# Attention and Fourier mixing on one core: the first batch's Fourier stage cut into halves, and the start of the program laid out anew

## The chip, the core and the metric

One core of a Trainium2 chip runs the whole program. The metric is the time of one execution in device microseconds, the median of several runs. The engines are TensorE (PE, with PEld for its weight loads), VectorE (DVE), ScalarE (ACT) and GpSimd (POOL); SyncE (SP) issues most of the DMAs. Each engine works through its own instructions in order and waits on semaphores for the others.

## What is computed

Two stages, in fp32 at input and output. First attention in chunks of 32 positions, each of which sees 8 memory keys, 16 positions to the left and 8 to the right; then a Fourier mixing of the result, and a two-layer network on the normalised sum:

```python
for c in range(S // 32):                       # q, k, v: (4, 8, 768, 64)
    k_full = concat([mem_k, k[c*32-16 : c*32+40]])
    a = softmax(q[c*32 : c*32+32] @ k_full.T / 8)
    attn[c*32 : c*32+32] = a @ v_full
x = attn.transpose(0, 2, 1, 3).reshape(4, 768, 512)
u = x + real(fft(fft(x, axis=1), axis=2))
un = (u - mean(u)) / sqrt(var(u) + 1e-6)
out = u + relu(un @ w_ch1) @ w_ch2             # (512, 2048), (2048, 512)
```

## The kernel before

**Attention.** The work goes in 16 units, four for each of the four batches; a unit `n` is a pair of heads. For a unit the kernel loads q, k and v (`qf`, `kf`, `va`, three buffers each), casts q and k to bf16 (`qb`, `kb`), turns each with eight TensorE transposes (`trq`, `trk`), and copies them out of PSUM (`qT`, `kTb`). Then come two halves `g` of six 64-position tiles each: scores `sc` (12 matmuls), exp into `e` on ScalarE, values `xa` (12 fp32 matmuls, 24 in the profile), and a normalisation on VectorE (`zs`, L360, and `xsb`, L361) into the batch's `xsb`. A key block is 96 wide: 8 memory keys, 16 left, 64 own, 8 right, on partitions 0 to 95. The pairs come in the order 0, 2, 1, 3, so that columns that are added to each other are there early.

**Fourier stage**, by batch (`fourier`, L646). The column sums and differences `zy` (L374), the row fold `pq` (L381, L382: the upper three row tiles plus and minus the lower three) and the column fold `ff` (L391, against a reversed copy) leave four parts (`par`, `ab`) of 128 columns each. ScalarE and VectorE split every part into two fp16 halves (`hi` L399, `lo` L404), and TensorE sums the rows against cosine and sine tables (`ps`, L414, 12 matmuls a part and 12 more for the middle column). The result is split again (`up` L426 and L430, `dn` L435), `pm` (L446) does the columns, VectorE adds and takes mean and variance (L452, L458), ScalarE subtracts the mean (`un`, L464), and `un` is turned, on TensorE for batch 0 (`tp`) and by a DMA for the others.

**Network**, by batch and half `sh`: `ph` (L497, 64 matmuls), a ReLU on ScalarE (L504), `pc` (L511, 48 matmuls), the sum `osb` (L517) and the store.

**Order.** Everything is a task of a planner (`Plan`, `plan.add`): an engine, a cost in us, the tasks it comes after, buffers that it takes and gives, a rank. `order` lets time run over these costs and starts on every engine the task of lowest rank that could start; the emitted program then has that order on every engine, whatever happens on the chip. Network tasks have very high ranks (`MLPS`), so they fill TensorE where nothing else can start. TensorE's costs count double before 40 us. The sine tables (`e_all_sines`) and the DMAs of the network's weights come after the exp of batch 0's last half (`x_last`). `xsb` has three buffers, so batch 3's attention waits for the end of batch 0's network.

Of the kernel before, what the change touches and what calls it, by code (L numbers as in the profile page):

```python
# [21 lines left out]
OWN = NMEM + LEFT  # L22
WIN = OWN + 64 + RIGHT

# [12 lines left out]
class Plan:  # L37
# [4 lines left out]
    LAG = {"PE": 0.2, "DMA": 2.0}  # L42

# [4 lines left out]
    def add(self, engine, cost, emit, after=(), take=(), give=(), rank=None, moved=0.0,  # L48
            loose=False):
        t = dict(engine=engine, cost=cost, emit=emit, after=[a for a in after if a is not None],  # L50
                 take=take, give=give, rank=len(self.tasks) if rank is None else rank,
                 moved=moved, done=None, at=None, no=len(self.tasks), loose=loose)
        self.tasks.append(t)
        return t

    def order(self):
# [8 lines left out]
        while any(waiting.values()):  # L65
# [4 lines left out]
            for e, ts_ in waiting.items():  # L70
# [3 lines left out]
                for t in ts_:  # L74
                    if held and not t["loose"]:
                        continue
                    if any(a["done"] is None or a["end" if a["engine"] == e else "done"] > now
# [11 lines left out]
                    cost = t["cost"] * (2.0 if e == "PE" and now < 40.0 else 1.0)  # L89
                    idle[e] = t["end"] = now + cost  # L90
                    if t["moved"]:
                        wire = max(wire, now + cost) + t["moved"]
                        t["done"] = t["end"] = wire + self.LAG["DMA"]
# [9 lines left out]
            if not moved:  # L103
                times = ([v for v in idle.values() if v > now] + [g[0] for g in gives]
                         + [t["done"] for t in placed if t["done"] > now])
# [8 lines left out]
def kernel(  # L114
# [41 lines left out]
    kf = [spool.tile([KP, 2, RB * D], FP32, name=f"kf{i}") for i in range(NS)]  # L156
    NV = 3
    va = [spool.tile([WIN, 2, NT, 66], FP32, name=f"va{i}") for i in range(NV)]
    NKT = 2
    kTb = [spool.tile([P, NT, WIN], BF16, name=f"kTb{i}") for i in range(NKT)]  # L160
# [27 lines left out]
    ident_b = cpool.tile([P, P], BF16)  # L188
    hpi_b = cpool.tile([P, 1], FP32)
# [4 lines left out]
    sinS = wpool.tile([P, 2, 3, NK], FP16)  # L194
    cosD = wpool.tile([P, 2, HD], FP16)
# [16 lines left out]
    def e_masks():  # L212
        nc.gpsimd.memset(mbias, 0.0)
        nc.gpsimd.memset(mbias[64:WIN, 0:1], NEG)
        nc.gpsimd.affine_select(out=mbias[0:64, 1:2], in_=mbias[0:64, 1:2],
                                compare_op=ALU.is_ge, fill=NEG, base=-(NMEM + CHUNK),
                                pattern=[[0, 1]], channel_multiplier=1)
        nc.gpsimd.memset(mbias[0:NMEM, 1:2], 0.0)
# [5 lines left out]
    def e_edges(i):  # L224
        v1 = va[i]
        nc.vector.memset(v1[:, :, :, D:D + 1], 1.0)
        nc.vector.memset(v1[0:32, :, 0, 0:D], 0.0)
        nc.vector.memset(v1[64:WIN, :, NT - 1, 0:D], 0.0)

    def e_edge_ones(i):  # L230
        v1 = va[i]
        lo, hi = v1[0:32, :, 0, D:D + 1], v1[64:WIN, :, NT - 1, D:D + 1]
        nc.gpsimd.affine_select(out=lo, in_=lo, compare_op=ALU.is_ge, fill=0.0, base=-OWN,
                                pattern=[[0, 2], [0, 1]], channel_multiplier=1)
        nc.gpsimd.affine_select(out=hi, in_=hi, compare_op=ALU.is_ge, fill=0.0,
                                base=OWN - 1, pattern=[[0, 2], [0, 1]], channel_multiplier=-1)
        nc.gpsimd.memset(v1[0:NMEM, :, 0, D:D + 1], 1.0)

    def e_kzero(i, lo, eng):
        r0, r1 = (0, KOFF) if lo else (QP, KP)  # L240
        eng.memset(kf[i][r0:r1].rearrange("p h e -> p (h e)"), 0.0)
# [10 lines left out]
    def e_load_qk(n, i):  # L252
        b, pr = seq[n]
        src, dst = ((q, qf), (k, kf))[i]
        r0 = KOFF * i
        nc.sync.dma_start(dst[n % NS][r0:r0 + QP],
                          src[b, 2 * pr:2 * pr + 2].rearrange("h (p j) d -> p h (j d)", j=RB))

    def e_cast(n, i, eng):
        src, of, rows, tag = ((qf, qb_of, QP, "qb"), (kf, kb_of, KP, "kb"))[i]  # L260
        of[n] = apool.tile([rows, RB, 2, D], BF16, tag=tag, bufs=1, name=tag)
# [3 lines left out]
    def e_load_v(n):  # L265
# [11 lines left out]
        for hh in range(2):  # L277
            run(NMEM, OWN - NMEM + 64, 1, NT - 1, 64 - LEFT, hh)
            run(OWN + 64, RIGHT, 0, NT - 1, 64, hh)
            nc.sync.dma_start(v1[0:NMEM, hh, :, 0:D],  # L280
# [16 lines left out]
    def e_turn_k(n):  # L297
        kb = kb_of.pop(n)
# [5 lines left out]
        for j in range(RB):  # L304
            nc.tensor.transpose(trk[:, j * KP:(j + 1) * KP],  # L305
                                kb[:, j].rearrange("p h d -> p (h d)"), ident_b[0:KP, 0:KP])

    def e_mkT(n):
        b, pr = seq[n]
        nc.vector.tensor_copy(  # L310
            kTb[n % NKT][:, :, 0:NMEM],
            mkT[:, b * HP + pr, :].unsqueeze(1).to_broadcast([P, NT, NMEM]))

    def e_kT(n):
        nc.scalar.copy(  # L315
            strided(kTb[n % NKT], NMEM, [[WIN, NT], [RB, 11], [1, RB]]),
            strided(tr_of.pop((n, 1)), 0, [[64 // RB, NT], [1, 11], [KP, RB]]))

    def e_scores(n, g):
        qT, kT = qT_of[n], kTb[n % NKT]  # L320
        sc_of[n, g] = sc = aps.tile([P, 2, 8, 64], FP32, tag="sc", bufs=1, name="sc")
        for t6 in range(6):
            t = 6 * g + t6
            for hh in range(2):
                r0 = 64 * hh
                nc.tensor.matmul(sc[0:WIN, hh, t6, :], kT[r0:r0 + 64, t, :],  # L326
# [3 lines left out]
    def e_exp(n, g):  # L330
        sc = sc_of.pop((n, g))
        e1_of[n, g] = e1 = apool.tile([WIN, 2, 6, 64], FP32, tag="e1", bufs=3, name="e1")
        for half in range(2):
            nc.scalar.activation(e1[:, :, :, ts(half, 32)], sc[0:WIN, :, 0:6, ts(half, 32)],  # L334
                                 AFT.Exp, bias=mbias[0:WIN, half:half + 1],
                                 scale=1.0 / math.sqrt(D))

    def e_values(n, g):
        e1 = e1_of.pop((n, g))
        if n < HP and g == 1:  # L340
            xa = fps.tile([P, 3, 2, 66], FP32, tag="mlp", name="xa")
        else:
            xa = aps.tile([P, 3, 2, 66], FP32, tag="xa", bufs=1, name="xa")
# [24 lines left out]
    mu_of, unT_of, rstd_of = {}, {}, {}  # L368
# [64 lines left out]
    def e_dn(b, par, ab):  # L433
        dn = fpool.tile([P, 2, HS], FP16, tag="dn", bufs=4, name="dn")
        nc.vector.tensor_copy(dn, rev_ap(up_of[b, par, ab][2], HS, HS, [[2 * NK, 2]]))  # L435
        up_of[b, par, ab][1] = dn

# [86 lines left out]
    t_zero = add("DVE", 0.2, e_zero)  # L524
    t_iota = add("POOL", 0.7, e_iota)
    t_mkf = add("ACT", 0.2, e_mkf, moved=0.8)
    t_id = add("POOL", 0.5, lambda: make_identity(nc, ident), rank=12)
    t_scales = add("DVE", 0.2, e_scales, [t_iota])
    t_kz, t_ones = {}, {}
    for i in range(NS):  # L530
        t_kz[i] = [add("DVE", 0.9, lambda i=i: e_kzero(i, 1, nc.vector), rank=-1) if i == 0 else
                   add("POOL", 0.9, lambda i=i: e_kzero(i, 1, nc.gpsimd), rank=17),
                   add("POOL", 0.9, lambda i=i: e_kzero(i, 0, nc.gpsimd),
                       rank=-1 if i == 0 else 17)]
# [248 lines left out]
```

## Time and profile before

| what | us |
|---|---|
| median of 3 runs (337.01 to 339.83) | 337.48 |
| the profiled execution, its own time | 336.54 |
| its span, first to last instruction | 334.8 |
| TensorE busy | 289.2 (86%) |
| VectorE busy | 177.3 (53%) |
| ScalarE busy | 164.6 (49%) |
| GpSimd busy | 48.9 (15%) |
| mean granted TensorE clock | 0.982 |

Shares are over the whole span, and the program has two unlike parts: up to some 80 us batch 0 goes through attention and Fourier stage, and after that TensorE has network work beside the other batches. In the rows of a timeline stand start, length, engine, line, operation, and in brackets how long the engine was idle before and for whom; in the chain of waits start, length and what ran; in the table by stretch each engine's busy time with its count, then the granted clock, the DMA share and GB/s.

### The profile page before, as it was taken

Reading aid. Unit: us, or ns where it says so; the run is one execution under the profiler, and the core shown is the slowest. Engines: PE = TensorE matmul, PEld = TensorE weight load, DVE = VectorE, ACT = ScalarE, POOL = GpSimd, SP = SyncE. Lnnn points to the kernel's source line nnn. Section 1 sums busy time; section 2 is a strip of 40 time slices with the busy share of each in tenths; the row PEclk is TensorE's granted clock in tenths of the full one; section 3 lists DMA queues with packets and bytes.
Section 4 is the critical chain, followed back from the end, with each engine's and each line's share of the span. In section 5 each row is a group of like instructions: output and inputs, shape, how many; then the busy total and the mean of one; then the engine's idle time right before and its main releaser. Section 6 shows DMA issues by size and latency. Waiting matters only on the chain.

```text
span 334.8 us, 6729 instructions
## 1 busy us (share of the span) xinstructions
PE 289.2 (86%) x2761; PEld 187.1 (56%) x2761; DVE 177.3 (53%) x341; ACT 164.6 (49%) x290; POOL 48.9 (15%) x66
## 2 busy tenths in 40 slices
PE   0585847798999997978999996889999999999995
PEld 0464746676666674656745654655455454554542
DVE  5944169988599894998923369790110200101001
ACT  1364488556796546758525623246345062250620
POOL 8201471013333024320001000000010000000000
PEclk9999999899999999979999999799999999999999
DMA  8999899994999196980054200100420100101001
GB/s 168 208 217 197 180 226 205 198 216 118 206 184 162 55 224 129 232 139 3 2 113 117 29 2 2 40 23 33 108 80 2 63 32 31 65 2 63 31 33 63
DMA packets 60287, 35.18 MB, mean 105 GB/s; under 512 B 48480, under 2 KB 50528, under 8 KB 60256
## 3 DMA queue, kind: packets, MB, share of 16 engines
q1 hardware_dynamic: 53824, 24.19, 38.8%
q0 software_dynamic: 2688, 4.19, 6.9%
q10 hardware_dynamic: 3744, 6.36, 5.1%
q8 instruction: 22, 0.36, 0.5%
q14 instruction: 9, 0.07, 0.1%
HBM read 30.28 MB, written 6.29 MB: 109 GB/s over the span
## 4 chain that ended last, share of the span: by engine, by line
PE 68%; DVE 16%; ACT 7%; DMA 4%; issue 1%; SPq 1%; POOL 0%; ACTq 0%; POOLq 0%; DVEq 0%
PE pc L511 24%; PE ph L497 22%; PE xa L350 7%; PE ps L414 6%; PE pm L446 4%; ACT e L334 3%; PE sc L326 2%; DVE ff L391 2%; DVE lo L404 2%; DVE zy L374 2%; DMA mkf<-in_mem_k_dram 1%; DMA qf<-in_q_dram 1%; DMA unT<-un 1%; DVE xsb L361 1%; DVE pq L381 1%
## 5 line engine op out<-in xcount | busy, mean ns | idle before, releaser
L497 PE MATMUL ph<-unT,w_sb 128*128 128x384 f16 x512 | 92.1, 326 | 1.7 <-ACT hT L504 1.2
L504 ACT ACTIVATE hT<-ph 128x384 f16<-128x384 f32 x128 | 60.9, 490 | 65.2 <-PE ph L497 65.1
L511 PE MATMUL pc<-w_sb,hT 128*128 128x512 f16 x384 | 85.8, 379 | 0.0
L517 DVE SCALAR_TENSOR_TENSOR osb<-pc,rstd,xsb 128x512 f32<-128x512 f32 x24 | 18.0, 749 | 101.7 <-PE pc L511 101.7
L497 PEld LDWEIGHTS <-w_sb 128*128 128x128 f16 x512 | 48.1, 97 | 35.1 <-issue 6.2
L511 PEld LDWEIGHTS <-hT 128*128 128x128 f16 x384 | 37.2, 98 | 42.6 <-issue 0.3
L334 ACT ACTIVATE e<-sc,mbias 96x384 f32<-96x384 f32 x64 | 33.4, 571 | 22.2 <-PE sc L326 21.5
L350 PE MATMUL xa<-va,e 96*64 96x65 f32 x768 | 35.3, 252 | 10.2 <-ACT e L334 9.4
L350 PEld LDWEIGHTS xa<-va,e 96*64 96x64 f32 x768 | 30.4, 162 | 17.4 <-ACT e L334 10.4
L464 ACT ACTIVATE un<-xsb,mu_s 128x512 f16<-128x512 f32 x24 | 17.3, 720 | 29.1 <-DVE mu_s L459 9.1
L262 POOL CAST qb<-qf 96x1024 bf16<-96x1024 f32 x12 | 14.2, 1184 | 82.1 <-DMA qf<-in_q_dram 82.1
L360 DVE RECIPROCAL zs<-xa 128x6 f32<-128x6 f32 x32 | 6.1, 192 | 31.2 <-PE xa L350 31.1
L414 PE MATMUL ps<-cosS,hi 128*128 128x193 f16 (+1 forms) x72 | 16.6, 282 | 4.8 <-DVE ff L391 3.2
L414 PE MATMUL ps<-cosS,lo 128*128 128x193 f16 (+1 forms) x72 | 16.4, 282 | 4.8 <-DVE lo L404 4.8
L326 PE MATMUL sc<-qT,kTb 64*96 64x64 bf16 x384 | 16.9, 228 | 3.8 <-ACT kTb L315 2.0
L426 ACT CAST up<-ps 128x386 f16<-128x386 f32 x16 | 9.6, 603 | 18.7 <-PE ps L414 18.6
L326 PEld LDWEIGHTS <-kTb 64*96 64x96 bf16 x384 | 13.2, 141 | 9.8 <-issue 4.7
L361 DVE TENSOR_TENSOR xsb<-xa,zs 128x384 f32<-128x384 f32 x32 | 17.8, 557 | 1.1
L315 ACT COPY kTb<-trk 128x1056 bf16<-128x1056 bf16 x16 | 16.6, 1036 | 3.7 <-PE trk L305 3.7
L374 DVE TENSOR_TENSOR zy<-xsb 128x768 f32<-128x768 f32 x16 | 17.4, 1098 | 0.3
L414 PEld LDWEIGHTS <-lo 128*128 128x128 f16 (+1 forms) x120 | 13.3, 110 | 7.2 <-DVE lo L404 6.4
L452 DVE TENSOR_TENSOR xsb<-pm,xsb 128x512 f32<-128x512 f32 x24 | 16.0, 667 | 2.2 <-PE pm L446 2.2
(86 smaller groups left out, 316.0 us busy)
## 6 DMA issues: line engine op xcount, KB each, us to landing
va<-in_v_dram SPq DMA_DIRECT2D x32, 220.0 KB
qf<-in_q_dram SPq DMA_DIRECT2D x16, 384.0 KB
kf<-in_k_dram SPq DMA_DIRECT2D x16, 384.0 KB
out_dram<-osb ACTq DMA_DIRECT2D x24, 256.0 KB
w_sb<-in_moe_w_ch_dram POOLq DMA_DIRECT2D x8, 512.0 KB, 15.8
va<-in_mem_v_dram SPq DMA_DIRECT2D x32, 24.0 KB
va<-in_v_dram SPq DMA_DIRECT2D x32, 22.0 KB
va<-in_v_dram SPq DMA_DIRECT2D x16, 32.0 KB
```

The lines of the kernel that those rows point to most:

```text
L315: nc.scalar.copy(strided(kTb[n % NKT], NMEM, [[WIN, NT], [RB, 11], [1, RB]]), strided(tr_of.pop((n, 1)), 0, [[64 // RB, NT], [1, 11], [KP, ...
L326: nc.tensor.matmul(sc[0:WIN, hh, t6, :], kT[r0:r0 + 64, t, :], qT[r0:r0 + 64, ts(t, 64)], start=True, stop=True, tile_position=(r0, 0))
L334: nc.scalar.activation(e1[:, :, :, ts(half, 32)], sc[0:WIN, :, 0:6, ts(half, 32)], AFT.Exp, bias=mbias[0:WIN, half:half + 1], scale=1.0 / ...
L350: nc.tensor.matmul(xa[64 * half:64 * half + 64, st, hh, 0:65], e1[:, hh, t6, :], v1[:, hh, 6 * g + t6, 0:65], start=True, stop=True)
L361: nc.vector.tensor_tensor(xs[b][:, 3 * g:3 * g + 3, 2 * pr * D:(2 * pr + 2) * D] .rearrange("p s (h d) -> p s h d", h=2), xa[:, :, :, 0:D] ...
L374: nc.vector.tensor_tensor(zy_of[b, par][:, :, c0:c0 + P], xb[:, :, c0:c0 + P], xb[:, :, HD + c0:HD + c0 + P], ALU.add if par == 0 else ALU ...
L414: nc.tensor.matmul(out_[:, sp, :], part[:, ab, sp * 3 + st, c0:c1], tab[:, sp, st, :], start=(st == 0 and i == 0), stop=(st == 2 and i == 1))
L464: nc.scalar.activation(un, xs[b][:, kt, :], AFT.Identity, bias=mu_of[b][:, kt, 0:1], scale=-1.0)
L497: nc.tensor.matmul(ph[:, 0:384], w1_sb[:, dt, ts(ht, P)], unT_of[b][:, dt, sh * 384:(sh + 1) * 384], start=(dt == 0), stop=(dt == NDT - 1))
L504: nc.scalar.activation(hT_of[b, sh][:, ht, :], ph_of.pop((b, sh, ht))[:, 0:384], AFT.Relu, bias=0.0, scale=-1.0)
L511: nc.tensor.matmul(pc_of[b, sh, stl], hT_of[b, sh][:, ht, ts(stl, P)], w2_sb[:, ht, :], start=(ht == 0), stop=(ht == NHT - 1))
L517: nc.vector.scalar_tensor_tensor(osb, pc_of.pop((b, sh, stl)), rstd_of[b][:, st:st + 1], xs[b][:, st, :], ALU.mult, ALU.add)
```

## The change

**Key blocks** are 128 wide. Partitions 0 to 31 of a block are zero, then 8 memory keys, 16 left, 64 own, 8 right. The zeros are written once (`va`, `kTb`), and the zero rows that the keys need at the edges come from a shifted identity (`turn_b`) and a cleared strip of a single `kb`, in place of cleared strips of three `kf`.

**Start.** GpSimd makes all casts of q and k. The angles of the tables come first on VectorE and the sines first on ScalarE; negated tables (`odd`, `nsinD`) are made on GpSimd. The kT copy of units 1 to 3 is on VectorE. The weights wait for the load of unit 3's v (`e_gate`). The values of batch 0 use one PSUM buffer instead of two and have later ranks.

**Batch 0's Fourier stage** (`first_fourier`) goes by row half `g` and column quarter: `g_zy` after units 0 and 1, a first fold step after unit 2, a second after unit 3, each of 3 row tiles. The row fold is not made; TensorE sums over both halves, with the table of odd frequencies negated for the second half, and the middle column has its own small part (`g_mid`). That is 120 row matmuls for 60.

**Planner.** A TensorE task that is not network work may be placed up to 0.7 us (`SLACK`) before its inputs are due, after 45 us; the double cost lasts until 45 us. ReLUs, output sums and stores have the lowest ranks instead of the highest.

```diff
+    FIRST = 45.0
+    SLACK = 0.7
...
+                    slack = (self.SLACK if e == "PE" and now > self.FIRST and not t["filler"]
+                             else 0.0)
...
+                           or (a["end"] > now if a["engine"] == e else a["done"] > now - slack)
...
-    kTb = [spool.tile([P, NT, WIN], BF16, name=f"kTb{i}") for i in range(NKT)]
+    kTb = [spool.tile([P, NT, P], BF16, name=f"kTb{i}") for i in range(NKT)]
...
+        nc.gpsimd.memset(v1[0:MEM0].rearrange("p h t c -> p (h t c)"), 0.0)
...
+    def g_ff(par, ab, g, last):
...
+        nc.vector.tensor_tensor(ff[:, :, 1:P], (ff if last else zy)[:, :, 1:P],
+                                rev_ap(xb, 2 * P - 1 + HD * last, P - 1, [[DM, 3]]),
+                                ALU.add if plus else ALU.subtract)
...
+    def g_rows(par, ab, g):
...
+        for sp in range(2):
+            tab = odd[:, ab] if g == 1 and sp == 1 else (cosS, sinS)[ab][:, sp]
...
+            part = [(ps[:, sp, :], g_hl(par, i)[:, ab, 3 * g + st, :], tab[:, st, :])
+                    for st in range(3) for i in range(2)]
...
-        ce, cn, cc = (nc.vector, "DVE", 0.68) if first else (nc.gpsimd, "POOL", 1.04)
+        cq, ck = [add("POOL", 1.1, lambda i=i, e=e: e_cast(n, i, nc.gpsimd), [e], take=(("qb", "kb")[i],),
...
-    t_sines = add("ACT", 6.2, e_all_sines, [t_angle["S"], t_angle["D"], x_last])
-    t_rows = add("DVE", 1.3, e_table_rows, [t_sines])
+    t_sines = add("ACT", 6.9, e_all_sines, [t_angle["S"], t_angle["D"]], rank=SINES)
+    t_neg = add("POOL", 1.4, e_negatives, [t_sines], rank=100)
+    t_rows = add("POOL", 1.8, e_table_rows, [t_sines, t_neg], rank=101)
...
+    t_gate = add("POOL", 0.1, e_gate, [t_lv[HP - 1]])
...
-    done = {0: fourier(0)}
+    done = {0: first_fourier()}
```

ScalarE at the start of the program, before (`trq` and `trk` are the turned q and k, `e` an exp; the sines stand after batch 0's last exp):

```order
L294 ACT_TABLE_LOAD
L294 COPY qT<-trq 128x768
L315 COPY kTb_85<-trk 128x12x88
L334 ACTIVATE e_225<-sc,mbias 96x12x32 x2
L334 ACTIVATE e_279<-sc,mbias 96x12x32 x2
```

and with the change:

```order
L710 ACT_TABLE_LOAD
L710 ACTIVATE sinS<-rS 128x579
L711 ACTIVATE cosS<-yS,hpi_b 128x579
L710 ACTIVATE sinS<-rS 128x579
L711 ACTIVATE cosS<-yS,hpi_b 128x579
L713 ACTIVATE sinD<-tri 128x512
L714 ACTIVATE cosD<-tri,hpi_b 128x512
L306 COPY qT<-trq 128x768
L326 COPY kTb_85<-trk 128x12x88
L306 COPY qT<-trq 128x768
L345 ACT_TABLE_LOAD
L345 ACTIVATE e_292<-sc,mbias 128x12x32 x2
```

All sines moved ahead of the first copy, one of the seven went to GpSimd, and the load of the exp's table stands after the second unit's qT.

GpSimd with the change, from the clear of the second `kTb` to the key cast of unit 1 (`_76`, `_79` are unit 0's buffers, `_77`, `_80` unit 1's); ahead of these rows stand the clears of `kb`, two `va` and the first `kTb`. In before its first cast is one of batch 1:

```order
L627 MEMSET kTb_86 128x1536
L274 CAST qb<-qf_76 96x2x8x64
L270 CAST kb<-kf_79 96x2x8x64
L244 AFFINE_SELECT va_84<-va_84 32x2
L246 AFFINE_SELECT va_84<-va_84 32x2
L249 MEMSET va_84 8x2
L250 MEMSET va_84 32x1584
L274 CAST qb<-qf_77 96x2x8x64
L270 CAST kb<-kf_80 96x2x8x64
```

The casts came over from VectorE, behind the clears, and TensorE's transposes of unit 1's keys, which wait for the last of these rows, stand ahead of its first scores.

VectorE at the end of batch 0's attention, before (from the last normalisation on):

```order
L360 RECIPROCAL zs<-xa 128x6
L361 TENSOR_TENSOR xsb_283<-xa,zs 128x3x128
L374 TENSOR_TENSOR zy<-xsb_283 128x6x128
L381 TENSOR_TENSOR pq<-zy 128x768
L382 TENSOR_TENSOR pq<-zy 128x768
L390 COPY ff<-pq 128x6
L391 TENSOR_TENSOR ff<-pq 128x6x127
```

and with the change, from the normalisation of unit 3's first half:

```order
L368 RECIPROCAL zs<-xa 128x6
L369 TENSOR_TENSOR xsb_341<-xa,zs 128x3x128
L471 TENSOR_TENSOR ff_552<-ff_552,xsb_341 128x3x127 x2
L497 TENSOR_TENSOR mid_114<-xsb_341 128x3
L499 CAST mid<-mid_114 128x3
L500 TENSOR_TENSOR mid<-mid_114,mid 128x3
L491 TENSOR_TENSOR lo_659<-ff_552,hi_658 128x384 x2
L368 RECIPROCAL zs<-xa 128x6
L369 TENSOR_TENSOR xsb_341<-xa,zs 128x3x128
```

The first half's folds and splits stand ahead of the last normalisation, and `pq` is gone.

276 lines of the change are left out of this document (196 added, 80 removed).

## The prediction

> **What bounds the kernel now.** I read the page first, for where TensorE is not full.
>
> ```profile
> span 334.8 us, 6729 instructions
> PE   0585847798999997978999996889999999999995
> DMA  8999899994999196980054200100420100101001
> ```
>
> A digit is 8.4 us. TensorE is loosely filled for nine slices, with the DMA engines full, and nearly solid after them. The chain of waits shows what each part is made of, and where the borders lie.
>
> ```profile
> 44.21 1.28 ACT L617
> 63.53 3.76 PE ps L414 x23
> 67.32 0.62 ACT up L426
> 78.88 0.65 PE ph L497 x4
> 310.05 10.40 PE ph L497 x64
> 320.45 10.37 PE pc L511 x48
> 330.85 0.75 DVE osb L517
> ```
>
> At 44.2 ScalarE begins on the sine tables: a table load of 1.28, seven activations, and a load back; batch 0's row sums end at 67.3, and the first MLP matmul starts near 78.7. From there the chain is mostly TensorE, up to 330.85, and 3.95 us of tail follow. So the time is the start of the MLP, plus the TensorE work still to do then, plus what TensorE loses, plus the tail. The work has these prices at full clock:
>
> ```profile
> 78.54 0.34 PE trq L289 x8
> 88.00 0.39 PE sc L326 x12
> 89.99 0.46 PE trk L305 x8
> 118.35 0.85 PE xa L350 x24
> 203.27 1.02 PE ps L414 x12
> 222.74 0.87 PE pm L446 x8
> ```
>
> In the order of before, after the first `ph` stand 21 groups of `xa`, 18 `sc`, 8 `trq`, 9 `trk`, 15 of twelve `ps`, 18 `pm`, 512 `ph` and 384 `pc`: 17.9+7.0+2.7+4.1+15.3+15.7+83.2+83.0 = 228.9, and under 1 for two `tp`: 229.7 us. The stretch is 330.85-78.7 = 252.2, so 22.4 us are lost in it. A table by stretch (TensorE's busy time is the number after the length), and the rows of the worst place, say where:
>
> ```profile
> 140.00:150.00 10.00, 7.61 (x85) 5.91 (x82) 9.35 (x11) 5.72 (x12) 3.96 (x3) 0.83 1.00 157
> 200.00:210.00 10.00, 6.65 (x53) 4.34 (x50) 9.85 (x16) 4.07 (x6) 0.00 (x0) 1.00 0.01 2
> 209.63 0.26 PE L414 MATMUL ps<-cosS,hi 128*128 128x193 f16 x1 [3.24 <-DVE ff L391]
> 210.63 0.34 PE L414 MATMUL ps<-cosS,lo 128*128 128x193 f16 x1 [0.73 <-DVE lo L404]
> ```
>
> The last batch's 60 row matmuls stand in one piece, with MLP work behind them: TensorE waits 4.0 us for VectorE, and then runs some 24 of them at half clock (163 ns each, 3.76 over 23, for 85), 1.9 us more.
>
> **The change, part by part.** I follow the path to the first `ph`.
>
> *Head.* GpSimd now casts all of q and k, and before that clears a `kb` strip, two `va` blocks (1584 elements) and two `kTb` (1536). Its nearest rows:
>
> ```profile
> 0.79 0.95 POOL L241 MEMSET kf<- 4x1024 f32 x1 [0.29 <-POOLq L767]
> 5.55 4.69 POOL L241 MEMSET kf<- 2x1024 f32 x4
> 13.65 1.04 ACT L334 ACTIVATE e<-sc,mbias 96x384 f32<-96x384 f32 x2 [0.86 <-PE sc L326]
> 14.75 1.57 PE L350 MATMUL xa<-va,e 96*64 96x65 f32 x24 [1.21 <-ACT e L334]
> 16.25 0.69 PE L326 MATMUL sc<-qT,kTb 64*96 64x64 bf16 x12
> 16.87 0.82 PE L289 MATMUL trq<-ident_b,qb 96*128 96x96 bf16 x8
> 17.92 0.79 ACT L294 COPY qT<-trq 128x768 bf16<-128x768 bf16 x1
> 19.58 0.85 PE L305 MATMUL trk<-ident_b,kb 100*128 100x100 bf16 x8
> 32.24 1.03 POOL L262 CAST qb<-qf 96x1024 bf16<-96x1024 f32 x1 [22.00 <-DMA qf<-in_q_dram]
> ```
>
> A memset costs 0.95 per 1024 elements, 1.17 in the row of four. Before reaches 5.55 with one such memset behind it; less that and the third `va` block's small pieces (0.6) it is 4.0. Then the strips take 0.95+2x1.47+2x1.42 = 6.7, so the first cast begins near 10.7; two casts (2.1), the third `va` block (2.0) and two casts more bring pair 1's key cast to about 17. If two-byte clears take half it is 15; with 1.17 for 0.95 and casts at 1.2, 20. TensorE has pair 1's `trk` ahead of the first scores, so they all stand behind that cast. Then `trk` 0.85, `trq` 0.82, the qT copy 0.8 (scores beside it), the Exp table 1.28, exp 1.04, second scores 0.69: `xa` starts at 22.5, where before has 14.75. The sines fill that hole: ScalarE has no copy to make until some 12 us. They cost nothing while VectorE has the angles by 10; each us later moves qT, and soon the path, by one.
>
> *Attention.* From there TensorE is the bound, at half clock:
>
> ```profile
> 34.15 1.50 PE xa L350 x24
> 35.65 0.64 PE sc L326 x10
> 25.32 0.69 DVE L262 CAST qb<-qf 96x1024 bf16<-96x1024 f32 x1 [3.64 <-DMA qf<-in_q_dram]
> 46.09 0.56 DVE L361 TENSOR_TENSOR xsb<-xa,zs 128x384 f32<-128x384 f32 x1
> 46.90 1.63 POOL L262 CAST qb<-qf 96x1024 bf16<-96x1024 f32 x1
> 47.67 1.67 DVE L381 TENSOR_TENSOR pq<-zy 128x768 f32<-128x768 f32 x1
> 63.67 0.94 DVE L404 TENSOR_TENSOR lo<-ff,hi 128x768 f16<-128x768 f32 x1
> L391 DVE TENSOR_TENSOR ff<-pq 128x762 f32<-128x762 f32 x16 | 15.0, 941 | 0.0
> ```
>
> Eight `xa` (12.0), six `sc` (3.8), five transposes (4.0), and 2.3 of standing for VectorE, since `xa` now has one PSUM buffer and the normalisation of 0.8 lies between: the last `xa` ends at 44.6. Before it ends at 45.8. The head's loss is won back because pair 2's values no longer stand behind a transpose that waits for batch 1's q, and the loads arrive in time (q of pair 3 landed at 25.3 in before).
>
> *Fourier stage.* The normalisation of pair 2's first half ends at 22.5 + 7.5 (five `xa`) + 2.6 (four `sc`) + 3.2 (four transposes) + 0.9 (itself) = 36.7. After it VectorE has sixteen half-size fold steps (0.5 each, 8.0), their small copies (1.2), eight `lo` (0.5 each, 4.0), the middle column (0.9) and three normalisations (2.3): 16.4, to 53.1. The casts of pair 5 fall on it. A cast took 1.63 instead of 1.03, and `pq` 1.67 instead of the 0.94 of `lo`, which has its size, when they met (rows above); I add 1, half of what three such meetings cost: 54. Before, the last `lo` ends at 64.6. The Trainium skill (SBUF — State Buffer, § Who interferes with whom) says that a VectorE operation with two SBUF inputs contends with a GpSimd instruction that reads SBUF, which speaks against casts on GpSimd here; the two stretched rows agree with it, and by it all folds that meet a cast pay, 2 us instead of 1. The kT copies of pairs 1 to 3, now VectorE's (ScalarE's took 1.0), fall before 36.7, where it waits for `xa`: nothing, or 1 where one stands ahead of a normalisation.
>
> The row fold `pq` is gone from VectorE and comes back as 60 more matmuls. TensorE starts the 120 at 45.6: 21 at half clock (3.5), 99 at 85 ns (8.4), scores and values of pair 4 between (1.3): 58.8, after VectorE's 54 plus 2, so TensorE is late next. If the clock stayed half throughout it would be 66. From the last row sum to the first `ph` before takes 78.7-67.3 = 11.4, of which two normalisations (0.75 each) drop out of VectorE's row: 10.2. The MLP starts at 69.0, 9.7 earlier.
>
> *Weights.* Their eight DMAs stand on GpSimd's queue behind a gate copy that waits for pair 3's v, and behind pair 4's casts; the casts of pair 5 stand behind them.
>
> ```profile
> L640 POOL DMA_DIRECT2D w_sb<-in_moe_w_ch_dram x4: 560/566/801, 41.5 to 43.4; - x4
> DMA to landing us min/median/max: 7.9/11.2/14.4
> ```
>
> Pair 4's keys are cast by 38; issued to 41 and 14.4 on the way, w1 is there at 55: hidden by 14 us.
>
> *After that.* The new order has 22 `xa`, 20 `sc`, 10 `trq` and 10 `trk` groups behind the first `ph`, 2.8 us more: 232.5. MLP work now stands between the pieces of the last batch's row sums, so the 5.9 us there should go; lost time 22.4-5.9 = 16.5, and 1.5 for waits that the planner's slack (0.7 us) now allows: 18. Key blocks of 128 columns: a scores group moves as many columns as before; if its loads grew by a third, 0.11 x 20 = 2.2 us; if they hide, nothing, and a faster load could give up to 1. I take nothing, since `trq` has 128-column loads already and eight of them fit with their matmuls into 0.34. Zero rows, exp on 128 partitions, tables on GpSimd: same lengths or beside other work, nothing.
>
> **Sum.** 69.0+232.5+18+3.95 = 323.4 of span. The profiled execution takes 336.54 for its span of 334.8, and the median is 0.94 above it: 323.4+1.74+0.94 = 326.
>
> **Rivals.** *The head eats the gain.* GpSimd at its worst prices and casts that meet VectorE's angle operations put pair 1's keys at 23; everything moves by 6, and with the stalls of the last batch kept (6) the result is 338, with half of either 332. For it: the clears already stretch from 0.95 to 1.17 in before. Against: the fold chain, not the attention, is the longer of the two, and part of a late head is lost in its waits. Within 1%: chance 0.14.
>
> *Planned waits (slower).* After 45 us the planner places a non-MLP TensorE step up to 0.7 us before its input is due, and the MLP matmuls stand behind it in order. Some 90 such steps come after the first `ph`. At 0.25 each on top of today's loss, 69+232.5+22.4+22.5+3.95 = 350, 353 as a median. It decides from 341: 10.5 us, 0.12 per step. Against: most inputs are there when TensorE reaches a step, and the slices of before from 84 to 126 us, with the same mix, all read 9. Chance 0.09.
>
> *TensorE warms early.* Dense row sums bring TensorE from 163 to 85 ns a matmul within before; the attention alone has not done it, since 24 `xa` at 44.24 still take 1.57 us after 5 us with gaps of 0.4 (the page shows a full clock there, which the durations contradict):
>
> ```profile
> 44.24 1.57 PE L350 MATMUL xa<-va,e 96*64 96x65 f32 x24 [0.45 <-ACT e L334]
> ```
>
> The new order has hardly a gap from 22 on; if that suffices, `xa` falls to 0.85, VectorE (25 us of folds, copies and normalisations from 24) bounds at 50, and the half-clock row sums go: 5 us less, 321. Chance 0.12. The Trainium skill (TensorE: Matmul & The Clock Gate, Part 1) gives some 3.4 us of sustained work as enough for the full clock; by it this rival would be the rule, and the row above speaks against it for attention work.
>
> **Numbers.** The forecast itself has 0.58 (317 to 333: 15 to 20 for the key cast is -2 to +3, half-clock row sums +7, the losses 12 to 24); a still better fill of later stages, below 316, 0.07. The range 316 to 338 leaves out that and the slow case. A measurement of this kernel tells about 1% from no change, 334.1 to 340.9. Faster: 0.58+0.12+0.07 = 0.77; same 0.14; slower 0.09.
>
> **What would show it.** Sines before 14 us; the first `xa` at 20 to 25; last `xa` of batch 0 near 45; last `lo` near 54; last row sum near 59; first `ph` at 66 to 72; no wait above 2 us at the last batch's `ps`. Wrong if the first `ph` is after 75, or if TensorE loses more than 25 us after it.

## The result, and the profile after

The changed kernel takes 320.25 us (median of 4 runs, 318.41 to 324.96) against 337.39 for the kernel before on the same chip: 0.946 of it, 95% interval 0.940 to 0.951. The forecast was 326, with a range of 316 to 338. Runs over 1.5% above the fastest of their kernel are left out of the ratios, two each of `oldfourier` and `neglate` below and one here: 324.96 us, at a granted clock of 0.976 where the others have 0.982 to 0.984. The profile that came with the result is of that execution, so the changed kernel is read below from the profile of its second measurement (execution 321.67, span 320.0).

The page first, the same three rows as of before:

```profile
span 320.0 us, 6896 instructions
PE   0128769889999799999999999999999999999994
DMA  9992999989955773939564310001600200101001
```

A digit is 8.0 us now. The loose stretch in front has nine digits, as before. After it one 7 is left, where before had two 7s, a 6 and four 8s. The borders, from the timeline of the first-layer matmuls and the end of the chain of waits:

```profile
L581 PE MATMUL ph<-unT,w_sb x64: 322/326/337, 74.1 to 89.9; 128*128 128x384 f16 x64
```

```profile
305.58 10.37 PE pc L595 x48
315.98 0.75 DVE osb L601
```

The network starts at 74.1 instead of 78.7, and the last `pc` ends at 315.98 instead of 330.85. With the prediction's prices 232.5 us of TensorE work stand between, so 315.98-74.1-232.5 = 9.4 us are lost after the start, against 22.4 before. So the end came 14.9 us sooner, and by these prices 13.0 of these came out of the lost time (2.2 of the 13.0 are in fact cheaper groups of scores, as the section after the experiments shows). The earlier start gave 4.6, of which the 2.8 us of extra work left behind it take back more than half. The forecast had it the other way round: 6.9 from the front, 4.4 from the lost time.

The two worst stretches of before, in the same table by stretch, for the changed kernel, with the next one, since most of its batch 2's folds stand there (before has them from 136 to 155):

```profile
140.00:150.00 10.00, 10.00 (x156) 6.10 (x153) 6.10 (x10) 6.68 (x12) 2.44 (x4) 1.00 0.93 174
150.00:160.00 10.00, 9.67 (x100) 6.15 (x99) 10.00 (x14) 5.49 (x10) 2.29 (x2) 1.00 0.55 155
200.00:210.00 10.00, 9.59 (x74) 6.58 (x74) 9.55 (x16) 7.33 (x15) 0.00 (x0) 1.00 0.07 26
```

TensorE was busy 7.61 of 10 us beside the folds of batch 2 and 6.65 beside those of batch 3; now it is busy 9.67 and 9.59, with VectorE about as full as before. In the changed kernel no row sum (`ps`) waits for VectorE; before, they waited 8.5 us for `lo` and `ff` in all.

The path to the first network matmul, as rows of the timeline (unit 1's key cast, the `xa` groups of batch 0 and a copy of memory keys on VectorE among them, the last `lo`, the late part of unit 4's `xa`, the last row sum):

```profile
18.59 1.05 POOL L270 CAST kb<-kf 96x1024 bf16<-96x1024 f32 x1
...
24.87 1.57 PE L358 MATMUL xa<-va,e 128*64 128x65 f32 x24
24.97 2.80 DVE L321 COPY kTb<-mkT 128x96 bf16<-128x96 bf16 x1 [3.14 <-PE sc L337]
...
28.60 1.57 PE L358 MATMUL xa<-va,e 128*64 128x65 f32 x24 [0.98 <-DVE xsb L369]
...
31.32 1.57 PE L358 MATMUL xa<-va,e 128*64 128x65 f32 x24
...
34.00 1.39 PE L358 MATMUL xa<-va,e 128*64 128x65 f32 x24
...
36.33 0.93 PE L358 MATMUL xa<-va,e 128*64 128x65 f32 x24 [0.20 <-PE trk L316]
...
39.39 0.92 PE L358 MATMUL xa<-va,e 128*64 128x65 f32 x24 [0.53 <-DVE xsb L369]
...
42.11 1.57 PE L358 MATMUL xa<-va,e 128*64 128x65 f32 x24 [1.52 <-issue]
...
45.94 1.57 PE L358 MATMUL xa<-va,e 128*64 128x65 f32 x24 [1.50 <-DVE xsb L369]
...
55.86 1.02 DVE L491 TENSOR_TENSOR hl<-ff,hl 128x384 f16<-128x384 f32 x2
...
58.31 0.80 PE L358 MATMUL xa<-va,e 128*64 128x65 f32 x20 [1.11 <-DMA va<-in_mem_v_dram]
...
62.98 0.67 PE L519 MATMUL ps<-odd,hl 128*128 128x193 f16 x6
```

Each stage is 2 to 5 us later than the prediction had it: key cast 19.6 (17), first `xa` 24.9 (22.5), last `xa` of batch 0 47.5 (44.6), last `lo` 56.9 (54), last row sum 63.6 (58.8), network 74.1 (69.0).

### The profile page after: what moved, and what is told of

Its sections match the earlier page's. It is cut to its first block, busy times and chain, and to the rows that moved or that the text cites. A ratio compares the mean times of both kernels' runs of the same rounds, so it can differ in the third digit from the quotient of the medians.

```text
span 323.3 us, 6896 instructions
## 1 busy us (share of the span) xinstructions
PE 283.6 (88%) x2821; PEld 181.1 (56%) x2821; DVE 175.7 (54%) x352; ACT 161.0 (50%) x289; POOL 72.6 (22%) x88
## 4 chain that ended last, share of the span: by engine, by line
PE 62%; DVE 13%; DMA 9%; POOL 6%; ACT 5%; issue 2%; SPq 1%; ACTq 0%; POOLq 0%
PE ph L581 23%; PE pc L595 21%; DMA va<-in_mem_v_dram 7%; PE xa L358 6%; PE pm L530 4%; PE ps L425 4%; DVE st L542 2%; DVE xsb L536 2%; DMA qf<-in_q_dram 1%; POOL va L250 1%; DVE osb L601 1%; PE trq L301 1%; PE sc L337 1%; ACT hi L410 1%; POOL qb L274 1%
## 5 line engine op out<-in xcount | busy, mean ns | idle before, releaser
L345 ACT ACTIVATE e<-sc,mbias 128x384 f32<-128x384 f32 x64 | 33.6, 577 | 23.0 <-PE sc L337 22.6
L358 PE MATMUL xa<-va,e 128*64 128x65 f32 x768 | 33.3, 242 | 7.4 <-DVE xsb L369 3.0
L358 PEld LDWEIGHTS xa<-va,e 128*64 128x64 f32 x768 | 28.6, 153 | 16.0 <-issue 10.6
L274 POOL CAST qb<-qf 96x1024 bf16<-96x1024 f32 x16 | 18.8, 1174 | 65.9 <-DMA qf<-in_q_dram 50.7
L270 POOL CAST kb<-kf 96x1024 bf16<-96x1024 f32 x16 | 22.6, 1411 | 13.7 <-PE trk L316 9.3
L301 PE MATMUL trq<-ident_b,qb 96*128 96x96 bf16 x128 | 9.7, 229 | 17.1 <-POOL qb L274 17.1
L306 ACT COPY qT<-trq 128x768 bf16<-128x768 bf16 x16 | 12.8, 800 | 12.9 <-PE trq L301 12.9
L369 DVE TENSOR_TENSOR xsb<-xa,zs 128x384 f32<-128x384 f32 x32 | 17.8, 557 | 1.1
L301 PEld LDWEIGHTS <-qb 96*128 96x128 bf16 x128 | 7.6, 110 | 18.3 <-POOL qb L274 17.2
L542 DVE BATCH_NORM_STATS2 st<-xsb 128x6 f32<-128x512 f32 x24 | 16.6, 693 | 0.7
L410 ACT CAST hi<-ff 128x768 f16<-128x768 f32 x12 | 10.0, 831 | 13.7 <-DVE ff L402 13.5
```

What stands on the lines that cost most here:

```text
L270: eng.tensor_copy(kb[0:QP].rearrange("p j h d -> p h j d"), src[n % NS].rearrange("p h (j d) -> p h j d", j=RB))
L274: eng.tensor_copy(of[n].rearrange("p j h d -> p h j d"), src[n % NS].rearrange("p h (j d) -> p h j d", j=RB))
L301: nc.tensor.transpose(trq[:, j * QP:(j + 1) * QP], qb[:, j].rearrange("p h d -> p (h d)"), ident_b[0:QP, 0:QP])
L345: nc.scalar.activation(e1[:, :, :, ts(half, 32)], sc[:, :, 0:6, ts(half, 32)], AFT.Exp, bias=mbias[:, half:half + 1], scale=1.0 / math.sqr ...
L358: nc.tensor.matmul(xa[64 * half:64 * half + 64, st, hh, 0:65], e1[:, hh, t6, :], v1[:, hh, 6 * g + t6, 0:65], start=True, stop=True)
L369: nc.vector.tensor_tensor(xs[b][:, 3 * g:3 * g + 3, 2 * pr * D:(2 * pr + 2) * D] .rearrange("p s (h d) -> p s h d", h=2), xa[:, :, :, 0:D] ...
```

## Experiments

Two questions were open. Which part of the change took the 13 us out of the lost time: the new front, the planner's slack, or its ranks? And what made the front late? All twelve runs, with the split of their profiled execution: the start of the first `ph`, the end of the last `pc`, the work between by the prediction's prices (the order of each kernel decides which groups are left), and what remains as lost. The time is the median of the runs that the ratio uses; the ratio is against the kernel before on the same chip, with its 95% interval.

| kernel | us | ratio | first ph | end | work | lost |
|---|---|---|---|---|---|---|
| before (first profile) | 337.5 | 1 | 78.7 | 330.85 | 229.7 | 22.4 |
| again (as changed) | 320.23 | 0.950 (0.946 to 0.955) | 74.1 | 315.98 | 232.5 | 9.4 |
| noslack | 321.19 | 0.954 (0.949 to 0.960) | 71.0 | 314.46 | 233.7 | 9.8 |
| oldranks | 335.24 | 0.995 (0.992 to 0.998) | 72.3 | 329.72 | 232.5 | 24.9 |
| oldplan | 337.11 | 1.000 (0.997 to 1.002) | 72.1 | 332.15 | 233.7 | 26.4 |
| osbold | 329.14 | 0.974 (0.970 to 0.978) | 71.0 | 321.93 | 232.5 | 18.4 |
| reluold | 321.34 | 0.953 (0.949 to 0.956) | 71.1 | 315.48 | 232.5 | 11.9 |
| planonly | 326.00 | 0.965 (0.961 to 0.969) | 84.0 | 320.46 | 228.0 | 8.5 |
| oldfourier | 329.30 | 0.975 (0.967 to 0.983) | 83.8 | 327.60 | 231.3 | 12.5 |
| head | 317.37 | 0.940 (0.937 to 0.944) | 70.5 | 311.36 | 232.5 | 8.4 |
| neglate | 319.88 | 0.947 (0.941 to 0.954) | 71.0 | 315.41 | 232.5 | 11.9 |
| wlate | 315.49 | 0.935 (0.931 to 0.939) | 71.0 | 309.29 | 232.0 | 6.3 |
| combo | 322.20 | 0.953 (0.949 to 0.957) | 71.1 | 316.93 | 232.0 | 13.8 |

Two cautions go with the table. The prices charge 0.39 us for a group of twelve scores, and with key blocks of 128 columns a group takes 0.28; so in every row but `before` and `planonly` some 2.2 us belong to the lost time and not to the work. And a split is of one execution: the other profile of the changed kernel, of the execution of 324.96, has the first `ph` at 75.7 and about 11 us lost, so these columns do not tell a difference of 1 or 2 us from chance.

**The changed kernel again.**

> The changed kernel once more, as it is. The prediction's split of the gain says: first network matmul near 69 us and about 18 us of TensorE time lost after it. The rival split, read from the profile that came with the result: first network matmul near 75 us, and about 11 us lost after it, so that the gain comes from later stages more than from the front. Time 318 to 321 us by both, since the medians are known; the place of the first network matmul decides.

Its rows stand above. The rival split holds: a network start at 74.1, not 69, and 9.4 us lost, not 18.

**No slack.**

```diff
-    SLACK = 0.7
+    SLACK = 0.0
```

> SLACK = 0: no TensorE step is placed before its inputs are due. If the slack is what keeps TensorE full in the later batches, the lost time after the first network matmul goes back from about 11 toward the 22 us of before: 325 to 331 us. By the prediction's step the slack costs 1.5 us of waits: 318 to 319 us. If it does neither, within 1 us of the changed kernel.

321.19, an interval that overlaps that of the changed kernel, and as little lost time (9.8). With the new ranks, no effect of the slack of 0.7 us shows, neither fuller nor emptier. The slower rival of the prediction, in which some 90 planned waits cost 0.25 us each, has no place left.

**Old ranks.**

```diff
     def RELU(i):
-        return i - MLPS
+        return MLPS + i
```

> ReLUs, output sums and stores have the highest ranks again, everything else as changed. If these ranks are what keeps TensorE full in the later batches, the time goes to 325 to 331 us, with ScalarE's ReLUs standing behind copies and exps and network matmuls waiting for them. By the prediction, which gave the ranks nothing, within 1 us of the changed kernel.

335.24: 15 us of the 17 are gone with this line, more than the expectation had for it. The lost time is 24.9, more than before the change. The table by stretch shows the place; the second fence has the second-layer matmuls (`pc`) alone, and the third the first output sum on VectorE in this stretch, from the timeline, all of the kernel with old ranks:

```profile
100.00:110.00 10.00, 7.68 (x109) 5.74 (x109) 10.00 (x15) 6.17 (x11) 1.88 (x2) 1.00 0.34 83
110.00:120.00 10.00, 7.57 (x110) 6.70 (x111) 8.77 (x19) 5.83 (x9) 0.46 (x1) 0.66 0.30 63
```

```profile
100.00:110.00 10.00, 2.06 (x9) 1.00 0.34 83
110.00:120.00 10.00, 0.00 (x0) 0.66 0.30 63
```

```profile
116.45 0.74 DVE L601 SCALAR_TENSOR_TENSOR osb<-pc,rstd,xsb 128x512 f32<-128x512 f32 x1
```

and the same two views of the changed kernel:

```profile
100.00:110.00 10.00, 5.49 (x24) 1.00 0.79 177
110.00:120.00 10.00, 0.37 (x2) 1.00 0.74 183
```

```profile
104.25 0.74 DVE L601 SCALAR_TENSOR_TENSOR osb<-pc,rstd,xsb 128x512 f32<-128x512 f32 x1
...
110.41 0.75 DVE L601 SCALAR_TENSOR_TENSOR osb<-pc,rstd,xsb 128x512 f32<-128x512 f32 x1 [1.00 <-PE pc L595]
```

With the old ranks VectorE is busy from 100 to 116 without a pause, for the most part with the folds and splits of batch 1. Its output sums come behind them, at 116.45; each of them gives back the PSUM buffer of a finished `pc`, and in the kernel's text `pc` and `ph` of this batch share two such buffers. So the planner has no network matmul to place (no `ph` runs from 100 to 120 either), TensorE waits for VectorE and ScalarE, and the granted clock of the second stretch falls to 0.66. With the new ranks an output sum goes between two folds at 104.25, and 24 `pc` matmuls stand in the gap. The price is 0.74 us of delay for the folds each time.

**Slack and ranks old together.**

> SLACK = 0 and the old ranks together, so that the planner's changes are gone but for the longer double cost (to 45 us) and the later due times of loads. If the later stages hold 8 or more of the 17 us, 328 us or more; if the front holds nearly all of it, 322 us or less. If slack and ranks repair the same losses, this run costs more than the two single ones together.

337.11, the time of the kernel before within its interval: the new front without the slack and the new ranks gains nothing (the longer double cost and the later due times of loads are still in). By the table it saves 2.6 us in start and work (72.1+233.7 against 78.7+229.7), and 4.0 more are lost later; with the scores at 0.28 it saves 4.9 and loses 6.3. Against the old ranks alone (335.24, on the same chip) the missing slack costs 1.9 us, by intervals that all but part.

**One rank at a time.** First the output sums and stores old, then the ReLUs:

```diff
                 os_ = add("DVE", 0.76, ...
-                          rank=RELU(len(plan.tasks)))
+                          rank=MLPS + len(plan.tasks))
...
                 add("ACT", 0.1, lambda st=st: e_out(b, st), ...
-                    rank=RELU(len(plan.tasks)))
+                    rank=MLPS + len(plan.tasks))
```

> The changed kernel, but with the old, highest ranks for the output sums and stores; the ReLUs stay first. The theory now: with old ranks for all three the time was 335.2 us, because in a batch's Fourier stage VectorE's output sums stand behind the folds, their PSUM buffers do not come free, and the planner has no network matmul to put between the row sums. If the output sums are the cause, 330 to 336 us. If the ReLUs are, 319 to 322 us.

```diff
                 relu.append(add("ACT", 0.5, ...
-                                rank=RELU(len(plan.tasks))))
+                                rank=MLPS + len(plan.tasks)))
```

> The changed kernel, but with the old, highest rank for the ReLUs; output sums and stores stay first. If the output sums carry the 15 us, 319 to 324 us. If the ReLUs carry them, 330 to 336 us: network matmuls then wait for ReLUs behind ScalarE's copies, casts and exps. If each carries a half, both kernels come out near 328.

329.14, just below what was expected of this cause, and 321.34: the output sums and stores carry 8 to 9 us by themselves (8.9 as the times stand, 8.0 by the ratios, since the kernel before took 0.7 us longer on that chip), the ReLUs about 1, which the intervals do not tell from nothing. Both together carry 15.0, so some 5 to 6 us appear only when both are old. Output sums and stores were changed together; which of these two it is was not tried, and the buffer argument above speaks for the sums.

**The planner alone, on the kernel before.** Slack and ranks as changed; the front, the costs of loads and the 40 us stay as in before.

```diff
+    SLACK = 0.7
...
     def RELU(i):
-        return MLPS + i
+        return i - MLPS
```

> The kernel before, with the planner's changes alone: slack 0.7 us, and lowest ranks for ReLUs, output sums and stores. Theory that the planner carries the gain by itself: the 22.4 us lost after the first network matmul fall to about 10, the front stays at 78.7: 324 to 327 us. Rival, that the ranks only work with the new front (whose planner changes alone undone gave the time of before): 333 us or more.

326.00. The old front with the new order of fillers loses 8.5 us after its start, though its network starts at 84.0 and not at the 78.7 that was expected to stay. So the planner is worth 11.9 us on the old front and 16.9 on the new one (337.11 to 320.23), and the front is worth nothing with the old order and 5 to 6 us with the new (5.8 by the times, 4.8 by the ratios).

**Old Fourier stage for batch 0.**

```diff
-    done = {0: first_fourier()}
+    done = {0: fourier(0)}
```

> The changed kernel with batch 0's Fourier stage as in the kernel before (row fold on VectorE, 60 row matmuls, no halves). By the prediction, which rested the earlier start on the fold chain: last `lo` 8 to 10 us later and the first network matmul near 82 instead of 74: 326 to 329 us. Rival: the fold chain is partly covered, since pair 4's scores and values and 1.7 to 5 us fewer of row matmuls stand in it: first network matmul near 77, 321 to 324 us.

Its four runs took 327.24, 331.35, 333.31 and 333.66, so the time is rough; the first two give 329.30, a ratio of 0.975 (0.967 to 0.983), at the upper end of what was expected. The profile is of the execution of 333.31. There the first `ph` starts at 83.8, 9.7 later than in the changed kernel, with 1.2 us less work behind it, which is the size that the prediction's fold chain implies, and 3.1 more are lost later. The halves of the Fourier stage are the part of the front that pays: without them the new front starts the network no earlier than the old one under the same planner (`planonly`, 84.0), and its time is no better (0.975 against 0.965, with intervals that touch).

**A shorter head.** Only the columns that stay zero are cleared; no order changes.

```diff
-    t_kTz = [add("POOL", 0.8, lambda i=i: nc.gpsimd.memset(kTb[i], 0.0), ...
+    t_kTz = [add("POOL", 0.5, lambda i=i: nc.gpsimd.memset(kTb[i][:, :, 0:MEM0], 0.0), ...
```

> The two `kTb` clears on GpSimd cover only the 32 columns that stay zero (384 elements instead of 1536), nothing else and no order changed. By the price of a clear (1.65 and 1.38 for 1536) they take about 0.4 each: unit 1's key cast ends near 17.4 instead of 19.6 and the first `xa` starts near 22.6 instead of 24.9. If the head sets the start of the network, the first network matmul comes 2 us earlier and the time is 317 to 319 us. If what ends later sets it (the load of unit 4's v, seen waited for by 1.1 to 2.7 us near 58), the first network matmul stays at 71 to 74 and the time at 319 to 321.

317.37, faster than the changed kernel (the intervals are apart). The timeline:

```profile
9.53 0.69 POOL L627 MEMSET kTb<- 128x384 bf16 x1
...
11.03 0.42 POOL L627 MEMSET kTb<- 128x384 bf16 x1
...
16.84 1.04 POOL L270 CAST kb<-kf 96x1024 bf16<-96x1024 f32 x1
...
23.11 1.57 PE L358 MATMUL xa<-va,e 128*64 128x65 f32 x24
...
44.20 1.57 PE L358 MATMUL xa<-va,e 128*64 128x65 f32 x24 [1.82 <-DVE xsb L369]
...
59.64 0.67 PE L519 MATMUL ps<-odd,hl 128*128 128x193 f16 x6
```

The first and the last `xa` of batch 0 come 1.8 us earlier, so the head does stand on the path up to there. The last row sum ends at 60.3 instead of 63.6, and of these 3.3 us 2.0 are there before the wait for `va` at 58, which is absent here (the twelve `ps` from `sinS` and `hl` begin at 52.74 instead of 54.75). But kernels with the long clears come close without a faster head: the last row sum ends at 60.4 in `noslack` and `wlate`, and at 60.8 in `osbold` and `reluold`, which have the front of the changed kernel, no wait for `va`, and row sums that reach the full clock (85 ns a matmul) at 49 instead of 52. Their first `ph` starts at 71.0 or 71.1, against 70.5 here. So the short clears move the network by 0.5 us beyond what other executions reach with the long ones; how much of the 2.9 us of the whole time is theirs stays open.

**Negated tables later.**

```diff
-    t_neg = add("POOL", 1.4, e_negatives, [t_sines], rank=100)
+    t_neg = add("POOL", 3.4, e_negatives, [t_sines, t_mk[2]], rank=100)
-    t_rows = add("POOL", 1.8, e_table_rows, [t_sines, t_neg], rank=101)
+    t_rows = add("POOL", 2.8, e_table_rows, [t_sines, t_neg], rank=101)
```

> The negated tables `odd` and `nsinD` stand on GpSimd behind the casts of unit 2 instead of ahead of them. Theory: the copy of 96 memory-key elements into `kTb`, which took 2.80 us on VectorE at 24.97 and held up the first normalisation, was slow because GpSimd worked beside it; with GpSimd idle it takes 0.2 to 0.4 us and the second `xa` starts 1 us earlier. Rival: the copy is long for another reason and stays above 2 us. The time changes by 1 us or less by both, since later waits take it up: 319 to 321.

In the changed kernel GpSimd was at work beside the copy of 96 elements, with casts among other things (its timeline):

```profile
25.71 1.03 POOL L274 CAST qb<-qf 96x1024 bf16<-96x1024 f32 x1
26.69 1.03 POOL L270 CAST kb<-kf 96x1024 bf16<-96x1024 f32 x1
27.74 1.04 POOL L274 CAST qb<-qf 96x1024 bf16<-96x1024 f32 x1
```

With the tables moved, one GpSimd cast starts as the copy does, and the copy takes 0.19 instead of 2.80 at the same place in the program (timeline of this kernel, VectorE, GpSimd and TensorE):

```profile
24.43 0.50 PE L337 MATMUL sc<-qT,kTb 64*128 64x64 bf16 x12 [0.87 <-ACT e L345]
24.86 1.57 PE L358 MATMUL xa<-va,e 128*64 128x65 f32 x24
24.97 0.19 DVE L321 COPY kTb<-mkT 128x96 bf16<-128x96 bf16 x1 [3.14 <-PE sc L337]
25.00 1.05 POOL L274 CAST qb<-qf 96x1024 bf16<-96x1024 f32 x1 [2.32 <-PE sc L337]
...
27.54 1.22 PE L358 MATMUL xa<-va,e 128*64 128x65 f32 x24
...
29.70 0.93 PE L358 MATMUL xa<-va,e 128*64 128x65 f32 x24 [0.66 <-PE sc L337]
```

The second `xa` starts 1.1 us earlier, and with no wait of TensorE from 24.4 on, it quickens within it. (The planner's order moved too: unit 2's transposes stand ahead of the second scores here.) The whole time is not shown to change: 319.88, with an interval that overlaps that of the changed kernel.

**Weights later.** Their DMAs wait for the load of unit 4's v instead of unit 3's.

```diff
-        nc.gpsimd.tensor_copy(gate[64:65], va[(HP - 1) % NV][64:65, 1, NT - 1, 0:1])
+        nc.gpsimd.tensor_copy(gate[64:65], va[HP % NV][64:65, 1, NT - 1, 0:1])
...
-    t_gate = add("POOL", 0.1, e_gate, [t_lv[HP - 1]])
+    t_gate = add("POOL", 0.1, e_gate, [])
...
+        if b == 1:
+            t_gate["after"].append(t_lv[HP])
```

> The eight DMAs of the network's weights wait for the load of unit 4's v instead of unit 3's, so they stand behind unit 4's casts and don't share the wire with that load. Theory: the wait for `va` near 58 (1.1 and 2.7 us in two profiles of the changed kernel, with 19 to 21 us for one load of 24 KB) goes, and `trq` of unit 4 no longer waits behind the issues near 41: first network matmul at 70 to 71, 317 to 320 us. Rival: the weights now end last; w1 takes up to 14.4 us, so if they are issued after 57 the first network matmul waits, 322 us or more.

315.49, the fastest of all and faster than expected: 4.7 us below the changed kernel, and 0.935 of before. In the changed kernel's chain of waits one load of 24 KB of unit 4's v stands for 19 us, beside the eight weight DMAs:

```profile
38.88 19.29 DMA va<-in_mem_v_dram
```

With the later gate no `xa` waits for it, the first `ph` starts at 71.0, and the weights, issued behind the casts of unit 4, are not waited for. But five kernels with the early gate (`noslack`, `osbold`, `reluold`, `head`, `neglate`) also start the network between 70.5 and 71.1 in their profiles, one of them with a wait for the same load (0.75 us, `neglate`). So the early start does not need the later gate. What sets this kernel apart is the 6.3 us lost after the start, against 8.4 to 11.9 in four of these five (`osbold`, with its old ranks, loses 18.4); the planner's whole order behind the gate changed with it, and how much of the 4.7 us is the load alone stays open.

**The three edits together.**

> The three edits together: short clears, negated tables later, weights behind unit 4's v. If each term of the head is on the path to the first network matmul, it starts near 67 to 68 and the time is 314 to 317 us. If VectorE's fold chain or a load sets it whatever stands ahead, 70 to 71, and the time is 318 to 320, as for the late weights alone.

322.20, outside both expectations: the edits do not add. The front is as good as with the late weights (71.1), but 13.8 us are lost later, 4.8 of them at one place. The waits of SP's queue there, and the timeline of SP, ScalarE's queue and TensorE:

```profile
SPq L292 <- DMA out_dram<-osb: 10.2, 1, 10.2
```

```profile
87.10 1.04 SPq L283 DMA_DIRECT2D va<-in_v_dram  x2
...
96.30 0.35 ACTq L605 DMA_DIRECT2D out_dram<-osb  x1
...
98.35 0.28 SPq L292 DMA_DIRECT2D va<-in_mem_v_dram  x1
...
99.99 0.32 SPq L264 DMA_DIRECT2D qf<-in_q_dram  x1
...
105.92 0.82 PE L301 MATMUL trq<-ident_b,qb 96*128 96x96 bf16 x8 [4.77 <-POOL qb L274]
```

Between two pieces of one v load SP stands for 10.2 us until a store has landed; the load of q, which stands behind, is issued at 99.99, and TensorE waits 4.77 us for its cast. The data of the two transfers have nothing to do with each other. That they share a semaphore would explain it, but it was not tried. The changed kernel and the one with the late weights alone have such waits too (up to 7.2 and 5.4 us); with the late weights alone TensorE waits for none of the casts behind them.

## Why the prediction was right, and where it was not

The sum fell by the right amount from the wrong places: 323.4 of span were forecast and 320.0 measured, 5.1 late at the start of the network, 8.6 better after it. That the two nearly cancel is luck. Of the signs that the prediction named, the sines, the first `xa` (24.9) and the last batch's row sums came as said, and the loss stayed under its 25; the last `xa`, `lo` and row sum of batch 0 came 3 to 5 us late, and the first `ph`, at 74.1, lies outside its 66 to 72 and just short of the 75 that would have made it wrong.

**The head** was priced at 17 for unit 1's key cast, 15 to 20 with its bounds; it ended at 19.6. It was near the upper bound, and "if two-byte clears take half" does not hold. GpSimd's clears in the timeline of the changed kernel, the `kb` strip of two-byte elements, one `va` block of four-byte ones and the two `kTb` of two-byte ones:

```profile
1.64 0.95 POOL L621 MEMSET kb<- 4x1024 bf16 x1
...
8.17 1.41 POOL L250 MEMSET va<- 32x1584 f32 x1
9.52 1.65 POOL L627 MEMSET kTb<- 128x1536 bf16 x1
...
12.01 1.38 POOL L627 MEMSET kTb<- 128x1536 bf16 x1
```

A clear is priced by its elements, not its bytes: the strip takes the same 0.95 as before's `kf` strip of as many four-byte elements. The first `xa` followed 5.2 us behind the cast's end (5.5 by the prediction).

**Tables on GpSimd "beside other work, nothing"** was wrong by one stall. `odd` and `nsinD` pushed the casts of unit 2 to 25.7, and the memory-key copy, which the prediction did not count at all, took 2.80 us beside them, ahead of the first normalisation. Moved apart, it takes 0.19. The price, of which the prediction's "nothing" should have been a bound, was 1.1 us at the second `xa`. The sentence of the Trainium skill that the prediction weighed was about operations with two inputs. The same section (SBUF — State Buffer, § Who interferes with whom) also names copies among the VectorE operations that can take the ports shared with GpSimd, and says that the one issued first blocks the other; the two lengths agree with that, though the copy here waited for more than one instruction.

**The clock.** The rival "TensorE warms early" came half true: `xa` takes 0.93 at 36.3, and 1.57 again at 42.1, after waits of 0.53 and 1.52 us among others, so the row sums began at half clock after all. The prediction argued from a row of before in which 5 us of attention with gaps of 0.4 had not brought the full clock. The neglate rows show what the objection missed: 3.1 us without a gap, and `xa` quickens from 1.57 to 1.22 and 0.93. In the changed kernel it took longer: its timeline has no wait from 28.60 to 36, `xa` still takes 1.57 at 31.32, and only in the group at 34.00, 5.4 us on, does it quicken. The rule that the prediction set aside (TensorE: Matmul & The Clock Gate, Part 1, of the Trainium skill: some 3.4 us of sustained work) is met by the first of these two and exceeded by the second.

**The Fourier stage.** The last `lo` came at 56.9 for 54, for the most part by the head's delay (54.9 in the run with the short clears). That TensorE would be late next was right: with the wait for `va` absent the last row sum ends at 60.3 to 60.8 (58.8), and the first `ph` starts 10.2 to 10.6 us behind it. The forecast has 10.2 there by a slip: 11.4 less two times 0.75 is 9.9, which would have made its start 68.7.

**Weights "hidden by 14 us"** was true for w1 itself and missed what they run beside: a load of 24 KB for unit 4 that landed 19 us after its issue, and for which `xa` waited 1.1 us. The network started 3 us later than in `noslack` and `reluold`, which have no such wait; in `reluold` the row sums also reached the full clock 3 us sooner, so the load has only part of these 3 us.

**After the start** is the term that was mis-sized most: "lost time 22.4-5.9 = 16.5, and 1.5 for waits that the planner's slack (0.7 us) now allows: 18". Measured 9.4 by the same prices, and 11.6 with the scores priced right. The 5.9 us of the last batch did go. But the prediction saw there only a better place for network work, and read the ranks of ReLUs, output sums and stores as no term of their own; undone, they take back 15 us. A smaller stall of the same kind stood in batch 2's Fourier stage, and not in the last batch's alone (7.61 of 10 at 140 before; 9.67 at 150 now). A still better fill of later stages stood among the chances, at 0.07 and without a mechanism; the runs supply it. The 1.5 us for the slack are not there.

**Key blocks of 128 columns** were taken at nothing, with 1 us as the best case. A group of twelve scores at full clock in the chain of waits of the changed kernel, the view from which the prediction took its 0.39:

```profile
35.39 0.28 PE sc L337 x12
```

0.28 against 0.39 is 2.2 us over the 20 groups behind the first `ph`, more than the best case. The load of a score's weights takes 99 ns in the mean where it took 141, so the loads neither grew nor hid: they became faster. The lost times above still charge 0.39.

## What to carry over

When a filler keeps the bound engine full, ask what gives the filler's buffers back, and on which engine that stands: 0.74 us output sums and their stores, placed behind a chain of folds, cost 8 to 9 us, and 15 together with the ReLUs, and ranks alone cured it. The faster front was worth nothing while the stretches behind it could not use it; the two are to be changed and measured together. And when a bulk load is moved earlier, look at the small loads that it now runs beside, not only at whether it arrives in time itself.

## What was not expected of the hardware

A VectorE copy of 96 two-byte elements took 2.80 us behind a row of GpSimd instructions and 0.19 where it started with GpSimd idle, a cast of 1.05 beginning 0.03 us after it. It was not held for one instruction alone: it was there from 24.97, GpSimd ran on through two casts of 1.03, and it ended at 27.77, as the second of them did. A clear on GpSimd costs by the element, whatever its width (1.38 to 1.65 us for 1536 two-byte elements, 1.41 to 1.93 for 1584 four-byte ones). A group of scores with 128 columns of keys takes 0.28 us and one with 96 took 0.39, by faster loads of weights; whether the width or the new layout of `kTb` does it was not tried. And a small load can take very long beside bulk transfers: 24 KB in 17.8 to 21.0 us, in four profiles.
